# Spectral filter with fused feed-forward: six filter-plane transfers, negation on VectorE, joined d remainders, and a tail inverse in four diagonal blocks

## The chip, the cores and the metric

The kernel runs on one core of one Trainium2 chip. The metric is the device time of one execution in microseconds (us), and less is better. A kernel's time is the median of several runs; beside them one execution is profiled, and all durations in this document that belong to single instructions come from profiled executions. The core has a matrix engine (TensorE, in the profile PE, with its weight loads shown apart as PEld), a vector engine (VectorE, DVE), an activation engine (ScalarE, ACT), GpSimd (POOL) and a synchronisation engine (SP). SP and POOL issue the DMA transfers here.

## The reference

The input `A_x` has 2048 rows (s) of 576 numbers (d), in bfloat16. Two layers follow each other:

```
h  = x + irfft2(rfft2(layernorm(x)) * (w_r + i w_i))
h2 = h + (gelu(layernorm(h) @ w_gate) * (layernorm(h) @ w_up)) @ w_down
```

The transform runs over both axes. The filter has 2048 x 289 complex numbers, held as two planes, `A_w_r` and `A_w_i`. The feed-forward part has an inner width of 4608. The result has the shape and type of `x`.

## The kernel before

Rows are split as s = 16 p + c: p is the SBUF partition (128 of them) and c is one of 16 tiles. Everything is written out in one program; a small class `Prog` derives the waits from the keys that each operation reads and writes, and every engine runs its own operations in the order in which they were recorded. For the spectral part that order is written out by hand in three strings (`SEQ1`, `SEQF`, `SEQ`), in which each word stands for one operation with its number.

**Stage A (`SEQ1`).** The 16 tiles of x arrive in five transfers. Statistics of the first layer norm are made per tile on VectorE (`B`, L464) or ScalarE (`S`, `Q`). The table ATB is scaled by the row's inverse deviation (`x`), and TensorE multiplies (`M`, L520) for five chunks k of d. Chunks 0 to 3 are 128 wide; they use the sums and differences of the two halves of d, for which POOL negates one half (`n`). Chunk 4 holds the remainder of d, two pieces of 32 numbers (256 to 287 and 544 to 575); its matmuls give 32 output partitions each, so that 64 partitions of U are filled, and the other 64 are zeroed once on POOL (L450). `E` copies a PSUM bank into U.

**Filter stage (`SEQF`).** There are 16 groups of rows of the spectrum, in the order of `GORD`. For each group:

- `D` (L574) makes the transform along d, six matmuls of 288 columns into two PSUM banks (odd and even columns of the spectrum, o = 0 and 1), three for each: two with 128-wide chunks and one with the remainder, 128 rows of which 64 are zero. One eviction on ScalarE writes CUS with columns interleaved.
- `B` (L584) finishes the transform along s: four matmuls, one eviction to YS on ScalarE.
- `T` (L594) multiplies on VectorE with the filter. For the complex product the filter buffer WS holds three planes per group: minus w_i, w_r and w_i.
- `Z` (L600, L603) adds the products on VectorE: 256 columns to ZS, the remaining 32 to ZR.
- `V` (L610) starts the inverse along s with four matmuls and an eviction to V on ScalarE.
- `R` (L620) does the same for the 32 remaining columns of up to four groups at once, and copies the result to VR, group by group, 32 partitions at a time (L565, VectorE and once ScalarE).

The filter planes come in 36 transfers, all issued by SP (`w_loads`, L428): for each plane, two halves of the groups, and in each half one transfer for every fourth row, with 72, 63 or 36 KB. The whole w_i plane is issued before w_r, behind the tables FT, BT and VT. POOL makes the negated plane, group by group (L632), once stage A's last scaled table is there, and then zeroes VR (L635). Behind that on POOL's queue stands the first load of gate weights, which has a buffer of its own and waits for nothing else; the other two gate and up slots share their memory with WS and wait for the last product.

**Inverse (`SEQ`).** For each of the first 8 tiles of rows `I` (L684) makes the inverse along d: for two halves h three matmuls of 288 columns, i = 0 and 1 from V, and i = 2, the tail, from VR. VR has 16 groups of 8 values, that is 128 weight columns, in which every 32-partition block is filled only for its own four groups; the rest is zero, and one matmul over 128 rows sums what is needed. `N` (L723) finishes the inverse along s and adds to x. The second layer norm follows, and TensorE transposes the first tiles (L777).

**Feed-forward.** Four blocks of 512 rows: gate and up (L824), 36 steps with 64-row matmuls on the two halves of the array, then down (L874), eight half-width passes of 36 matmuls. In the first block's down part the inverse of the other 8 tiles is done: `def_i` (L841) ahead of each half-width pass, eight matmuls of 144 columns, four from V and four from VR, and `def_n` (L855) at f == 22. Between them stand one ScalarE copy (L844) and four VectorE operations (L848 to L851).

Banks of PSUM for D, B, V and R are given out by the small loop from L550.

Of the kernel before, what the change touches and what calls it, by code (L numbers as in the profile page):

```python
# [12 lines left out]
NZ = 5  # L13
NVZ = 15
# [9 lines left out]
SEQ1 = """k14 B0 B1 v0 Q2 S2 B3 q0 v1 n0 n2 c0 q1 S4 x0D c1 M0 E1A B6 E0A Q4 B5 B7 x1P v2 E2D n1 B8 E3A E4A k104 M1 q2 c2 B9 Q10 E5A E7A n3 v3 S10 B12 E6A q3 c3 x2P B11 k202 M2 E9A x3P Q13 v4 E12A E8A q4 n4 B14 c4 B15 E10A E11A S13 E13D M3 E14A E15A v5 x4P E16D q5 E17A c5 E18A M4 n5 x5D E20D E19A E22D E21A M5 E23D E24A E25A E27A E26D E29A E28D""".split()  # L24
ACT_TILES = tuple(int(w[1:]) for w in SEQ1 if w[0] == "Q")
SEQF = """D0 D1 B0 D2 D3 T0 B1 D4 T1 B2 Z0 Z1 D5 T2 Z2 B3 D6 T3 B4 T4 D7 B5 Z4 D8 Z3 V0 B6 T5 Z5 T6 V1 B7 V3 Z6 T7 D9 R0 B8 D10 V2 Z7 D11 T8 B9 V6 B10 Z8 T9 R1 B11 V4 Z9 D12 D13 V5 T10 B12 T11 Z10 V7 B13 Z11 T12 T13 D14 R2 V9 D15 B14 V8 B15 Z12 V10 Z13 V13 V11 T14 Z14 V12 V14 T15a T15b Z15b Z15a R3 V15 R4""".split()
RENG = [['dve', 'dve', 'dve', 'dve'], ['dve', 'dve', 'dve', 'dve'], ['dve', 'dve', 'dve', 'act'], ['dve', 'dve', 'dve'], ['dve']]
# [13 lines left out]
def build_tables():  # L41
# [7 lines left out]
    T = {}  # L49
    n1 = np.arange(128)[:, None]  # L50
# [17 lines left out]
    I = I.reshape(4, 16, 2, 16, 128).transpose(1, 0, 2, 3, 4)  # L68
# [12 lines left out]
    fr = np.zeros((6, 128, 2, HK))  # L81
    dr = np.concatenate([np.arange(256, 288), np.arange(544, 576)])
    for o, kk in enumerate((k2o, k2e)):
        for h, fn in enumerate((np.cos, np.sin)):
            for t in range(2):
                fr[3 * o + t, :, h] = fn(ang(np.arange(128 * t, 128 * t + 128), kk))
            fr[3 * o + 2, 0:64, h] = fn(ang(dr, kk))
# [220 lines left out]
def _build(nc, A_x, A_w_r, A_w_i, B_w_gate, B_w_up, B_w_down, out):  # L308
# [16 lines left out]
    WS = sb.alloc("WS", [128, NG, 3, KW], BF16)  # L325
# [3 lines left out]
    VR = sb.alloc("VR", [128, NT, 2, NG, 8], BF16)  # L329
# [38 lines left out]
    FT = sb.alloc("FT", [128, 6, 2 * HK], BF16)  # L368
# [47 lines left out]
    x_load(0, 0, 2)  # L416
    x_load(1, 2, 4)
    atb_load(0, 0, 4)
    x_load(2, 4, 8)
    atb_load(1, 4, 8)  # L420
    x_load(3, 8, 12)
    x_load(4, 12, 16)
    atb_load(2, 8, 16)
    P.dma(SP, FT[:, :, :].rearrange("p a b -> p (a b)"), dram["FTAB"][:, :], "ft", w=["FT"])
    P.dma(SP, BT[:, :, :, :].rearrange("p a b c -> p (a b c)"), dram["BTAB"][:, :], "bt", w=["BT"])
    P.dma(SP, VT[:, :, :, :].rearrange("p a b c -> p (a b c)"), dram["VTAB"][:, :], "vt", w=["VT"])

    def w_loads(pl, hf, eng):  # L428
        g0, g1 = ((1, 9), (9, 16))[hf]
        src = (A_w_r, A_w_i)[pl]  # L430
        o = []
        for jj in range(4):
            o.append((WS[jj:64:4, g0:g1, 1 + pl, :], 1 + (16 * jj + g0) * K2, [[128 * K2, 16], [K2, g1 - g0], [1, K2 - 1]], jj))
            o.append((WS[64 + jj:128:4, g0:g1, 1 + pl, :], 1 + (64 + 16 * jj + 16 - g0) * K2, [[128 * K2, 16], [-K2, g1 - g0], [1, K2 - 1]], 4 + jj))
        if hf:
            for p0 in range(2):
                o.append((WS[64 * p0:64 * p0 + 64, 0, 1 + pl, :], 1 + 64 * p0 * K2, [[128 * K2, 16], [16 * K2, 4], [1, K2 - 1]], 8 + p0))
        return [lambda d=d, off=off, ap=ap, h=h: P.dma(eng, d, bass.AP(src.tensor, off, ap), f"w{pl}{hf}", w=[("W", hf, pl, h)]) for d, off, ap, h in o]

    for f in w_loads(1, 0, SP) + w_loads(1, 1, SP) + w_loads(0, 0, SP) + w_loads(0, 1, SP):  # L440
        f()
    GORD = list(range(1, NG)) + [0]
    wkeys = [[("W", hf, pl, h) for pl in range(2) for h in range(8 + 2 * hf)] for hf in range(2)]
# [6 lines left out]
    P.op(POOL, lambda g: g.memset(U[64:128, 4, :, :, :], 0.0), w=["Uz"])  # L450
# [56 lines left out]
    def a_mm(i):  # L507
        c0, c1 = GROUPS[i]
        for k in AORD:
            b = a_bank(i, k)  # L510
            for c in range(c0, c1):
                o = 128 * (c - c0)
                if k == 4:
                    parts = [(XO[:, c, 256 + 288 * h:288 + 288 * h], 32 * h, 32 * h + 32, True, True) for h in range(2)]
                else:
                    d0 = 128 * (k // 2)
                    x2 = XN[:, c, d0:d0 + 128] if k % 2 else XO[:, c, 288 + d0:416 + d0]
                    parts = [(XO[:, c, d0:d0 + 128], 0, 128, True, False), (x2, 0, 128, False, True)]
# [4 lines left out]
    def a_ev(n, eng):  # L523
        i, k = n // 5, AORD[n % 5]
        c0, c1 = GROUPS[i]
        n, b, w = c1 - c0, a_bank(i, k), 64 if k == 4 else 128
# [18 lines left out]
    P.alias([("XN", c) for c in range(NT)], [("V", g, c) for g in range(NG) for c in range(2)])  # L545
    uk = [[("U", i, k) for i in range(len(GROUPS))] + (["Uz"] if k == 4 else []) for k in range(5)]
# [4 lines left out]
    for t, w in enumerate(SEQF):  # L551
# [5 lines left out]
        elif k in "VR":  # L557
            b = min((6, 7) if ("D", LAST) not in FB else range(8), key=lambda b: used[b])
            used[b] = t + 1
        else:  # L560
            continue
# [6 lines left out]
    def st_D(i, eng=ACT):  # L568
        g = GORD[i]
        b0, s3 = FB["D", i], i % 3  # L570
        for o in range(2):
            b = b0 + o
            for m, us in enumerate((1 - o, 3 - o, 4) if o == 0 else (4, 1 - o, 3 - o)):
                P.op(PE, lambda t, b=b, m=m, us=us, o=o, g=g: t.matmul(bank(b, 0, 128, 0, 2 * HK), U[:, us, g, :, :], FT[:, 3 * o + (2 if us == 4 else us // 2), :], start=(m == 0), stop=(m == 2)),  # L574
                    r=uk[us] + ["FT"], w=[("PS", b)])
        ev(eng, CUS[:, s3, :, :].rearrange("p a (j r) -> p r a j", r=2), banks(b0, 2, 2 * HK).rearrange("p r (a j) -> p r a j", a=2),
           [("PS", b0), ("PS", b0 + 1)], [("CU", s3)])
# [10 lines left out]
    def st_T(i, q0=0, q1=KW, hs=(0, 1)):  # L588
        g, sl = GORD[i], i % 2
# [5 lines left out]
             r=[("Y", sl), ("Wn", i)] + wkeys[0 if 1 <= g < 9 else 1], w=[("T", sl, h) for h in hs])  # L595

    def st_Z(i, hs=(0, 1)):
# [3 lines left out]
        if 1 in hs:  # L601
            q, j = (i // 4 % 2, i % 4) if i < LAST else (0, 0)
# [3 lines left out]
    def st_V(i, b=6, eng=ACT):  # L606
        g, z3, sp_ = GORD[i], i % NZ, 1 if GORD[i] == 0 else 0
        for c in range(2):
            for zp in range(2):
                P.op(PE, lambda t, b=b, c=c, zp=zp, sp_=sp_, z3=z3: t.matmul(bank(b, 0, 128, 256 * c, 256 * c + 256), ZS[:, z3, zp, c:256:2], VT[:, sp_, zp, :],  # L610
                                                                            start=(zp == 0), stop=(zp == 1)), r=[("Z", z3), "VT"], w=[("PS", b)])
        for k0, k1, e in ((0, 4, eng),) if eng is not None else ((0, 2, ACT), (2, 4, ACT)):
            ev(e, V[:, :, k0:k1, g, :].rearrange("p n k e -> p k n e"), bank(b, 0, 128, 128 * k0, 128 * k1).rearrange("p (k n e) -> p k n e", k=k1 - k0, n=16),
               [("PS", b)], [("V", g, k) for k in range(k0 // 2, k1 // 2)])

    def st_R(q, engs, b=7):
        js = [i for i in range(4 * q, 4 * q + 4) if i < LAST] if q < 4 else [LAST]
        sp_, n = (1, 32) if q == 4 else (0, 32 * len(js))
        for zp in range(2):
            P.op(PE, lambda t, b=b, zp=zp, n=n, q=q, sp_=sp_: t.matmul(bank(b, 0, n, 0, 256), ZR[:, q % 2, zp, 0:n], VT[:, sp_, zp, :], start=(zp == 0), stop=(zp == 1)),  # L620
                 r=[("ZR", q % 2, j) for j in range(len(js))] + ["VT"], w=[("PS", b)])
        for j, i in enumerate(js):
            ev(engs[j], VR[32 * j:32 * j + 32, :, :, GORD[i], :].rearrange("p n k e -> p k n e"), bank(b, 32 * j, 32 * j + 32, 0, 256).rearrange("p (k n e) -> p k n e", k=2, n=16),
               [("PS", b), "Vz"], [("V", GORD[i], 2)])
# [6 lines left out]
    for i in range(NG):  # L631
        P.op(POOL, lambda v, g=GORD[i]: v.tensor_scalar(WS[:, g, 0, :], WS[:, g, 2, :], -1.0, 1.0, op0=ALU.mult, op1=ALU.mult),  # L632
             r=[k for k in wkeys[0 if 1 <= GORD[i] < 9 else 1] if k[2] == 1] + [("ATS", NT - 1)], w=[("Wn", i)])
        if i == NVZ:
            P.op(POOL, lambda g: g.memset(VR[:, :, :, :, :], 0.0), w=["Vz"])  # L635
    for w in SEQF:
        i = int(w[1:].rstrip("abc"))
        if w[0] == "D":
            st_D(i)
        elif w[0] == "B":  # L640
            st_B(i)
# [7 lines left out]
        elif w[0] == "V":  # L649
            st_V(i, FB["V", i], ACT if i < LAST else None)  # L650
# [21 lines left out]
    vk = [[("V", g, c) for g in range(NG)] for c in range(3)]  # L672
    vkeys = vk[0] + vk[1] + vk[2] + ["Vz"]
# [8 lines left out]
    def i_mm(c, h, i):  # L682
        b, kt = SLOT["I", c] + h, 2 * i + h
        P.op(PE, lambda t, b=b, h=h, i=i, kt=kt, c=c: t.matmul(bank(b, 0, 128, 0, KW), (V[:, c, kt, :, :] if kt < 4 else VR[:, c, kt - 4, :, :]), DT[:, 3 * h + i, 0:KW],  # L684
                                                              start=(i == 0), stop=(i == 2)), r=vk[i] + ["DT"], w=[("PS", b)])
# [151 lines left out]
    def def_i(c):  # L837
        for o in range(2):
            for t_ in range(2):
                for i, ch in enumerate((o, 2)):  # L840
                    P.op(PE, lambda t, o=o, t_=t_, i=i, ch=ch, c=c: t.matmul(bank(2 + o, 0, 128, HK * t_, HK * t_ + HK), (V[:, c, 2 * ch + t_, :, :] if ch < 2 else VR[:, c, t_, :, :]),  # L841
# [106 lines left out]
```

## Time and profile before

| What | Value |
|---|---|
| Median of 3 runs | 496.52 us (495.99 to 497.1) |
| Profiled execution | 496.66 us |
| Its span, first to last instruction | 494.9 us |
| TensorE busy | 486.1 us (98%) |
| VectorE, ScalarE, GpSimd busy | 192.4, 158.9, 34.6 us |
| Stage A | to 20.0 us |
| Filter stage | 20.0 to 52.44 us |
| First product with the filter | 27.26 us |
| Inverse and second layer norm | 52.44 to 64.77 us |
| Gate and up, first block | 64.77 to 134.8 us |
| Down with deferred inverse | 134.8 to 176.2 us |

A row of the groups gives the source line, the engine, the operation, the tile written and those read, partitions x elements, the count, then busy time and the mean of one in ns, then the engine's idle time ahead of it and what ended it. For matmuls, 128*32 means 128 rows of the array and 32 weight columns. Starts are recorded; matmul ends are modelled, so a matmul's "mean" contains its way through the array, and the step from one start to the next is the better measure of its cost. A row of the chain or timeline gives the start, the length and what ran.

### The profile page before, as it was taken

How to read it: one execution, taken by the hardware profiler on the slowest of the kernel's cores; microseconds unless marked ns; L12 is line 12 of the kernel's file. 1: busy time of each engine (PE TensorE's matmuls, PEld its weight loads, DVE VectorE, ACT ScalarE, POOL GpSimd, SP SyncE). 2: the span in 40 equal slices, each digit the busy share in tenths (PEclk: the TensorE clock that was granted, in tenths of full speed). 3: DMA queues.
4: the chain of work that ended last, by engine and by line, in shares of the span. 5: the costliest groups of instructions: out<-in, count | busy, mean ns of one | idle time of the engine just before them, and what ended most of it. 6: DMA issues, size and time to landing. Idle time of an engine off the chain costs nothing.

```text
span 494.9 us, 9880 instructions
## 1 busy us (share of the span) xinstructions
PE 486.1 (98%) x4338; PEld 288.1 (58%) x4338; DVE 192.4 (39%) x418; ACT 158.9 (32%) x300; POOL 34.6 (7%) x53
## 2 busy tenths in 40 slices
PE   7999999999999999999999999999999999999998
PEld 3767655555588854444477744444677544444775
DVE  6679743444365644433311144333211233333111
ACT  6989865232312243232300033232100132233000
POOL 5750701000000010000000000000000000000000
DMA  8666898411000062000000001000000000000000
GB/s 276 163 188 215 277 350 275 178 25 27 4 13 13 19 191 60 19 9 1 1 13 19 18 15 23 19 1 1 7 19 12 14 1 1 1 1 2 12 19 19
DMA packets 27164, 31.26 MB, mean 63 GB/s; under 512 B 11664, under 2 KB 20112, under 8 KB 27120
## 3 DMA queue, kind: packets, MB, share of 16 engines
q1 hardware_dynamic: 24224, 18.68, 13.0%
q0 software_dynamic: 2896, 11.95, 7.1%
q8 instruction: 34, 0.56, 0.5%
q14 instruction: 10, 0.08, 0.1%
HBM read 26.28 MB, written 2.36 MB: 58 GB/s over the span
## 4 chain that ended last, share of the span: by engine, by line
PE 88%; DVE 4%; issue 1%; ACT 0%; DVEq 0%
PE PS L824 57%; PE PS L874 29%; DVE TP L594 1%; DVE VR L565 1%; PE PS L841 1%; PE PS L684 1%; PE PS L723 1%; DVE ZS L600 1%; DVE XO L726 0%; PE PS L855 0%; DVE ZR L603 0%; PE PS L610 0%; DVE HN L757 0%; PE PS L777 0%; DVE TM L734 0%
## 5 line engine op out<-in xcount | busy, mean ns | idle before, releaser
L824 PE MATMUL PS<-HT,WG 64*128 64x512 bf16 x2106 | 228.5, 376 | 0.0
L824 PEld LDWEIGHTS PS<-HT,WG 64*128 64x128 bf16 x2106 | 107.3, 94 | 119.8 <-issue 1.0
L833 ACT ACTIVATE GL<-PS 128x512 bf16<-128x512 f32 x144 | 85.9, 597 | 257.3 <-PE PS L824 243.4
L834 DVE TENSOR_TENSOR AT<-GL,PS 128x512 bf16<-128x512 bf16 x144 | 98.9, 687 | 175.0 <-ACT GL L833 175.0
L874 PE MATMUL PS<-WD,AT 128*128 128x288 bf16 (+2 forms) x1152 | 144.3, 286 | 0.0
L874 PEld LDWEIGHTS PS<-WD,AT 128*128 128x128 bf16 x1152 | 110.8, 98 | 30.7 <-ACT GL L833 1.3
L877 DVE TENSOR_TENSOR OS<-PS,XO 128x288 bf16<-128x288 f32 (+2 forms) x32 | 14.6, 457 | 100.3 <-PE PS L874 100.3
L824 PE MATMUL PS<-HT,WGX 64*128 64x512 bf16 x486 | 53.4, 376 | 0.0
L824 PEld LDWEIGHTS PS<-HT,WGX 64*128 64x128 bf16 x486 | 23.7, 94 | 28.8
L714 ACT ACTIVATE JD<-XO 128x576 bf16<-128x576 bf16 x8 | 5.5, 683 | 28.5 <-DVE XO L858 28.5
L594 DVE TENSOR_TENSOR TP<-YS,WS 128x1152 bf16<-128x1152 bf16 (+2 forms) x17 | 11.8, 715 | 6.8 <-DMA WS<-in_A_w_r_dram 6.7
L574 PE MATMUL PS<-FT,U 128*128 128x288 bf16 x96 | 14.1, 286 | 0.1
L565 ACT ACTIVATE CUS<-PS 128x576 bf16<-128x576 f32 x16 | 13.5, 862 | 0.5 <-PE PS L574 0.4
L565 ACT ACTIVATE YS<-PS 128x576 bf16<-128x576 f32 x16 | 11.3, 705 | 2.3 <-DVE TP L594 2.2
L520 PE MATMUL PS<-ATS,XO 128*128 128x128 bf16 (+1 forms) x128 | 10.1, 221 | 1.7 <-POOL XN L534 1.1
L584 PE MATMUL PS<-CUS,BT 128*128 128x288 bf16 x64 | 10.5, 286 | 1.2 <-ACT YS L565 0.9
L464 DVE BATCH_NORM_STATS2 ST<-XO 128x6 f32<-128x288 bf16 x24 | 9.3, 438 | 4.5 <-DMA XO<-in_A_x_dram 4.5
L574 PEld LDWEIGHTS PS<-FT,U 128*128 128x128 bf16 x96 | 9.1, 98 | 2.9 <-ACT CUS L565 0.4
L520 PEld LDWEIGHTS PS<-ATS,XO 128*128 128x128 bf16 (+1 forms) x128 | 7.4, 97 | 4.7 <-POOL XN L534 1.6
L610 PE MATMUL PS<-VT,ZS 128*128 128x256 bf16 x64 | 9.0, 273 | 1.1 <-DVE VR L565 0.5
L565 ACT ACTIVATE V<-PS 128x512 bf16<-128x512 f32 (+1 forms) x17 | 10.0, 639 | 0.3 <-PE PS L610 0.2
L757 DVE TENSOR_SCALAR HN<-XO,TM,RS 128x576 bf16<-128x576 bf16 (+1 forms) x32 | 10.0, 361 | 0.0
(77 smaller groups left out, 215.0 us busy)
## 6 DMA issues: line engine op xcount, KB each, us to landing
WD<-in_B_w_down_dram POOLq DMA_DIRECT2D x9, 576.0 KB, 21.4
WG<-in_B_w_gate_dram POOLq DMA_DIRECT2D x4, 1152.0 KB, 9.7
WG<-in_B_w_up_dram SPq DMA_DIRECT2D x4, 1152.0 KB, 7.9
out_dram<-OS SPq DMA_DIRECT2D x30, 72.0 KB, 1.6
XO<-in_A_x_dram SPq DMA_DIRECT2D x3, 576.0 KB, 7.4
WGX<-in_B_w_gate_dram POOLq DMA_DIRECT2D x1, 1152.0 KB, 6.9
WGX<-in_B_w_up_dram SPq DMA_DIRECT2D x1, 1152.0 KB, 10.8
HT<-HN SPq DMA_TRANSPOSE x60, 2.4
```

What stands on the lines that cost most here:

```text
L464: P.op(DVE, lambda v, c=c, h=h: v.bn_stats(ST1[:, c, h, :], XO[:, c, 288 * h:288 * h + 288]), r=[("X", c)], w=[("ST1", c, h)])
L520: P.op(PE, lambda t, b=b, lhs=lhs, p0=p0, p1=p1, s=s, e=e, o=o, c=c: t.matmul(bank(b, p0, p1, o, o + 128), lhs, ATS[:, c, :], start=s, sto ...
L565: fn = (lambda v: v.tensor_copy(dst, src)) if eng == DVE else (lambda a: a.activation(dst, src, ACTF.Copy))
L574: P.op(PE, lambda t, b=b, m=m, us=us, o=o, g=g: t.matmul(bank(b, 0, 128, 0, 2 * HK), U[:, us, g, :, :], FT[:, 3 * o + (2 if us == 4 else u ...
L584: P.op(PE, lambda t, b=b, tb=tb, m=m, s3=s3, sp_=sp_: t.matmul(bank(b, 0, 128, 0, KW), BT[:, sp_, tb, :], CUS[:, s3, m, :], start=(m == 0) ...
L594: P.op(DVE, lambda v: v.tensor_tensor(TP[:, sl, :, :, q0:q1], y4, w4, op=ALU.mult), r=[("Y", sl), ("Wn", i)] + wkeys[0 if 1 <= g < 9 else ...
L757: P.op(eng, lambda v, c=c, hs=hs, o0=o0, o1=o1, x0=x0, x1=x1: v.tensor_scalar(HN[:, hs, o0:o1], XO[:, c, x0:x1], TM[:, 1, c:c + 1], RS2[:, ...
L824: op = P.op(PE, lambda t, h0=h0, kt=kt, wt=wt, b=b, s=(not second and j == 0), e=(second and j == n - 1): t.matmul(bank(b), wg_tile(slot)[ ...
L833: P.op(ACT, lambda a: a.activation(GL[:, s2, :], bank(b0), ACTF.Gelu_apprx_tanh), r=[("PS", b0)], w=[("GL", s2)])
L834: P.op(DVE, lambda v: v.tensor_tensor(AT[:, f, :], GL[:, s2, :], bank(b0 + 1), op=ALU.mult), r=[("GL", s2), ("PS", b0 + 1)], w=[("AT", f)])
L874: P.op(PE, lambda t, b=b, d0=d0, d1=d1, f=f, p=p: t.matmul(bank(b, 0, 128, 0, d1 - d0), AT[:, f, 128 * p:128 * p + 128], WD[:, f, d0:d1], ...
L877: P.op(DVE, lambda v, b=b, d0=d0, d1=d1, p=p, c=c: v.tensor_tensor(OS[:, p % 2, d0:d1], bank(b, 0, 128, 0, d1 - d0), XO[:, c, d0:d1], op=A ...
```

## The change

- **Six transfers.** Each filter plane is loaded in three: partitions 0 to 63 for slots 0 to 15, partitions 64 to 127 for slots 16 down to 1, and partitions 0 to 63 for slot 16. WS has 17 slots; the groups in their order use slots 1 to 16. SP issues w_i before w_r within each part, ahead of VT.
- **Negation on VectorE.** The words `w0` to `w3` negate w_i for four groups at a time. POOL no longer negates the plane. Each product waits for all six transfers and for its negation.
- **One pair of row halves.** Stage A writes the d remainder twice, to partitions 0 to 63 and 64 to 127 (four 32-column matmuls per tile instead of two). D then begins with two matmuls on 64 rows, lower for o = 0 and upper for o = 1, and goes on with four full ones. FT has five planes instead of six, and POOL no longer zeroes part of U. The D eviction writes in order and reads PSUM interleaved.
- **Tail in four diagonal blocks.** V and VR hold the groups in the order `GSLOT`, and ITAB is permuted to fit. VR holds only each block's own four groups, a quarter of its former size, without zeroes; R copies all groups of a set in one operation. The tail of the inverse, `I` at i = 2 and `def_i` at ch = 2, becomes four matmuls with 32 rows and 32 weight columns, from partitions 32 j to output partitions 32 j.
- **Order and engines.** `SEQ1`, `SEQF` are new; six statistics passes on ScalarE instead of eight. D0, B10 and V14 are evicted by VectorE; R2 and R3 by ScalarE. V15 goes to two banks.

```diff
-    for i in range(NG):
-        P.op(POOL, lambda v, g=GORD[i]: v.tensor_scalar(WS[:, g, 0, :], WS[:, g, 2, :], -1.0, 1.0, ...), ...)
-        if i == NVZ:
-            P.op(POOL, lambda g: g.memset(VR[:, :, :, :, :], 0.0), w=["Vz"])
+    def st_w(i):
+        g0, g1 = 4 * i + 1, 4 * i + 5
+        P.op(DVE, lambda v: v.tensor_scalar(WS[:, g0:g1, 0, :], WS[:, g0:g1, 2, :], -1.0, None, op0=ALU.mult), r=wkeys[1], w=[("Wn", 4 * i + k) for k in range(4)])
...
+    def w_load(pl, part):
+        src = (A_w_r, A_w_i)[pl].tensor
+        if part == 0:
+            dst, ap = WS[0:64, 0:NG, 1 + pl, :], bass.AP(src, 1, [[128 * K2, 16], [K2, 64], [1, K2 - 1]])
+        elif part == 1:
+            dst, ap = WS[64:128, NG:0:-1, 1 + pl, :], bass.AP(src, 1 + 64 * K2, [[128 * K2, 16], [K2, 64], [1, K2 - 1]])
+        else:
+            dst, ap = WS[0:64, NG, 1 + pl, :], bass.AP(src, 1, [[128 * K2, 16], [16 * K2, 4], [1, K2 - 1]])
+        P.dma(SP, dst, ap, f"w{pl}{part}", w=[("W", pl, part)])
+    for part in range(2):
+        for pl in (1, 0):
+            w_load(pl, part)
+    for pl in (1, 0):
+        w_load(pl, 2)
...
     def st_D(i, eng=ACT):
+        for m in range(3):
+            for o in range(2):
+                p0, p1 = (0, 128) if m else (64 * o, 64 * o + 64)
+                us, fs = (2 * m - 1 - o, 2 * o + m - 1) if m else (4, 4)
...
-                    parts = [(XO[:, c, 256 + 288 * h:288 + 288 * h], 32 * h, 32 * h + 32, True, True) for h in range(2)]
+                    parts = [(XO[:, c, 256 + 288 * (h % 2):288 + 288 * (h % 2)], 32 * h, 32 * h + 32, True, True) for h in range(4)]
...
     def i_mm(c, h, i):
+        for p0, p1 in [(0, 128)] if i < 2 else [(32 * j, 32 * j + 32) for j in range(4)]:
+            lhs = V[:, c, kt, :, :] if i < 2 else VR[p0:p1, c, h, :, :]
...
     def def_i(c):
+                    for p0, p1 in [(0, 128)] if ch < 2 else [(32 * j, 32 * j + 32) for j in range(4)]:
+                        lhs = V[:, c, 2 * ch + t_, :, :] if ch < 2 else VR[p0:p1, c, t_, :, :]
```

## The prediction

> **What bounds the kernel now.** I read the chain of work that ended last in order of time, then busy time by stage, the waits, both DMA queues, and groups by shape.
>
> The chain (start us, length us, what):
>
> ```profile
> 40.56 0.41 DVE VR L565
> ...
> 49.91 0.74 DVE TP L594 x2
> ...
> 52.44 1.63 PE PS L684 x12
> ...
> 64.77 70.11 PE PS L824 x648
> 134.88 0.61 PE PS L841 x8
> 135.48 2.69 PE PS L874 x22
> ```
>
> After 64.77 us the chain is TensorE without a gap, so each nanosecond added to its stream there is added to the end. From 27.26 to 52.3 us the chain lies mostly on VectorE (products L594, sums L600/L603, remainder copies L565), then on TensorE in the inverse (L684, L723). Busy time of each engine in the head, filter, inverse and first gate/up stage:
>
> ```profile
> 20.00:27.26 7.26, 7.00 (x58) 5.17 (x56) 0.56 (x2) 5.52 (x9) 6.14 (x14) 1.00 0.43 91
> 27.26:52.44 25.18, 22.66 (x182) 16.57 (x181) 24.54 (x63) 23.71 (x43) 5.86 (x6) 1.00 0.62 194
> 52.44:64.77 12.33, 11.82 (x100) 8.61 (x101) 9.92 (x34) 10.19 (x24) 7.91 (x11) 1.00 1.02 364
> 64.77:134.81 70.04, 70.04 (x649) 36.55 (x649) 27.35 (x51) 26.94 (x46) 1.28 (x2) 1.00 0.42 136
> ```
>
> Columns after the length: PE, PEld, DVE, ACT, POOL. In the filter stage all three compute engines are nearly full, DVE most; in the inverse PE has 0.51 us of slack; then none. VectorE does nothing from 20.5 to 27.26 because of one wait, whose cause is SP's issuing, 18 small transfers per plane at about 0.64 us each:
>
> ```profile
> DVE TP L594 <- DMA WS<-in_A_w_r_dram: 6.7, 1, 6.7
> ```
> ```profile
> 19.51 12.57 SPq L218 DMA_DIRECT2D WS<-in_A_w_r_dram  x18
> ```
>
> The matmuls to be split, by shape, and what stage A shows of a change of array shape:
>
> ```profile
> L684 PE MATMUL PS<-DT,VR 128*128 128x288 bf16 x16 | 4.5, 286 | 0.0
> L841 PE MATMUL PS<-DP,VR 128*128 128x144 bf16 x32 | 4.8, 226 | 0.0
> ```
> ```profile
> 7.47 0.22 PE L520 MATMUL PS<-ATS,XO 128*128 128x128 bf16 x1
> 7.53 0.22 PE L520 MATMUL PS<-ATS,XN 128*128 128x128 bf16 x1
> 7.68 0.29 PE L520 MATMUL PS<-ATS,XO 128*32 128x128 bf16 x4
> ```
>
> Full matmuls start 0.056 us apart; the first with 32 columns starts 0.149 after the last full one. The trace's own starts give 95 to 99 ns beyond streaming at each of the 20 changes that no other wait disturbs: 128x128 to 128x32 (7) and back (6), 64x128 to 128x128 (4, one of them at the first L841), 128x128 to 64x128 (3). The matmul after a change back starts a further 10 ns late.
>
> **What the Trainium skill says.** "TensorEngine Tiling (Array Packing)", Key Properties: changing the tiling mode, not just the tile, drains TensorE. The trace agrees, 95 to 99 ns. "TensorE: Matmul & The Clock Gate", Part 3: tiles on different row groups run together, about 4 ns apart. The trace agrees for two: 3 to 4 ns between the 128x32 ones of a pair, 3 to 20 ns between 64-row halves; four diagonal blocks it does not show. "SBUF — State Buffer", Door 1: a transfer to 64 partitions reaches 8 of 16 ports, 196 GB/s at 1 MiB. The new transfers have 64 partitions or fewer. The nearest measurement is the drain of queued plane rows at 14.5 to 16.5 us, about 402 rows of 576 B per us = 232 GB/s, both halves mixed. "DMA: Bandwidth & Descriptors", Issuing engines are not separate DMA queues: SP's and POOL's transfers share the engines. The trace agrees: while POOL's gate load flowed (32 to 35 us, 337 GB/s) the last two w_r transfers, issued at 30.8 and 31.5, waited and landed at 37.3 and 38.1.
>
> **Part by part.**
>
> *Transfers.* 36 plane issues become 6; at 0.65 us SP is through them by about 10.5 us instead of 32. The bound becomes the data: 4,224 rows, 2.43 MB. FT and BT land near 14.4; by then perhaps 900 rows have come (525 before, plus the time of VT's 256 KB, now queued behind, and FT's 72 KB less). The other 3,300 need 8.2 us at 402 rows/us or 9.7 at 196 GB/s: 22.6 to 24.1, and 0.5 us to complete. But POOL loses 16 negations (8.2 us with gaps) and the 3.5 us memset, so its queue comes to the first gate load after x_neg 5, at about 17.5 us instead of 30.1; 1.33 MB start flowing some 1.7 us later and take 3.3 us at 400 GB/s, shared with the rows. So the last plane lands between 23.1 (no sharing) and 28 (all 3.3 us, low rate); I take 26.5. VT follows within a microsecond, and the inverse tables soon after (41.8 us before).
>
> *Negation on VectorE.* w0 stands ahead of T0 and waits for the whole w_i plane. Four planes at once, 1,152 elements: the nearest row is tensor_scalar 128x576 at 425 ns, so 0.45 to 0.6, I take 0.5. T0 starts at 27.0 (23.6 to 28.5) against 27.26: the large stall mostly remains. Queued behind w0 are only products, for which ACT's YS and then PE wait, as before.
>
> *VectorE after T0.* Before: 25.7 us almost without a gap. New: products 16 x 0.68 = 10.9, sums 16 x 0.53 = 8.5, remainder copies 3 x 0.43 = 1.3 instead of 6.4, w1 to w3 1.5, B10 0.7, V14 0.65: 23.6. So 2.1 of work goes. ACT sheds two evictions there and takes R2, R3 at 0.38. The CUS eviction now reads PSUM strided and writes in order; the trace has no such form: 0.65 us (YS row, same size) to 0.2 slower than today's 0.86 mean. At 9 evictions after T0 that is 1.8 us on about 21, still under VectorE.
>
> *Forward d remainder.* Per D: two full matmuls (0.244) become a 64-row pair (0.126), but two shape changes (0.194) and the 10 ns: +0.086, x16 = +1.4 us of PE, 0.8 of it after T0 (9 D's). PE there goes from about 20.6 to 21.5 us, under VectorE's 23.6, so hidden; without that cover it costs the 0.8. In stage A four 128x32 pieces per tile replace two, together in the array: nothing but a few ns each; PE is not its bound. The U memset (1.8 us) hid under the x loads. ACT there has 6 statistics passes and 25 copies for 8 and 22; a shorter stage A goes into the wait for the planes.
>
> Filter sum: 0.3 earlier plus 2.1 less, with 0.6 given back as three full engines wait for each other: -1.8 (from -5 to +1).
>
> *Inverse tail.* Each of 16 remainders in the inverse (L684 row) and 32 in the deferred inverse (L841 row) becomes an excursion to four 32x32 blocks: in 0.095, blocks as long as the one matmul plus 3 x 0.004, out 0.097, 0.010 after: 0.214 us. Inverse: 16 x 0.214 = 3.4, less 0.4 of PE's slack: +3.0. Deferred: 32 x 0.214 = 6.85, all in a stage with no PE gap: +6.9. If blocks start 20 ns apart, as some halves do, 48 x 0.048 = 2.3 more. The EB/QB/YB chain to the f == 22 matmuls shifts along and stays in its cover.
>
> Sum: -1.8 + 3.0 + 6.9 = +8.1 on the profiled span 494.9, 503.0. The profiled execution took 496.66 (1.76 outside the span), the median is 496.52: 504.6.
>
> **The rivals.**
> *Four blocks one after another*: they write one PSUM bank. Then 3 x 0.122 x 16 = 5.9 and 3 x 0.062 x 32 = 6.0 more: 516.5. For it: unseen here; against it: the pairs seen in one bank (128x32) run together.
> *Planes no earlier, filter not shorter*: the rows crawl behind the gate load, T0 at 28.5, filter +1: 507.4. For it: the w_r transfers at 37 us.
> *No drain for the blocks* (other side): small weights load behind running full matmuls, an excursion costs 0.012. Then D gains instead of losing (0.2 of it after T0), inverse and deferred pay 48 x 0.012 = 0.6: -1.8 - 0.2 + 0.6 = -1.4, or with the planes at 23.6 and the filter 5 shorter -4.6: 491.9 to 495.1. It decides when an excursion costs under about 0.046 us, (1.8 + 0.4 of slack)/48. Against it: every shape change in the trace pays 95 ns or more.
>
> **How the numbers follow.** Main case 0.73 (504.6, own range 500.5 to 508.5), serial blocks 0.07, late planes 0.10, no drain 0.10. The range 500.3 to 509 holds most of the main case (0.70) and of the late planes (0.09). About 0.2% (1 us) is what measurement tells from no change: no drain gives faster 0.08 and same 0.02, the main case's far tail 0.01 of same; slower 0.89.
>
> **What would show it.** Each L841 group of a deferred half taking 1.35 us instead of 0.5, gaps of 0.095 at each 32-row block, the inverse 15.3 us long instead of 12.3, the first product near 27 behind an SP queue empty since 11, first inverse matmul near 50.6, gate/up blocks still 70.04. Wrong if the blocks start without a gap, or if the planes land by 23.5 and the filter gives 5 us.

## The result and the profile after

The changed kernel takes 509.47 us (median) against 496.54 us: ratio 1.0258 [1.0238, 1.0278], slower. The prediction was 504.6 us with a range of 500.3 to 509.0, so the direction is right and the time lies just above the range. One execution of the changed kernel had TensorE at about a quarter of its speed throughout (1,805 us); the profile shown here is that of the next measurement of the same kernel (509.52 us, ratio 1.0261 [1.0246, 1.0276]). Its span is 507.3 us, in an execution of 509.12 us.

Busy time by stage, after: head up to the landing of the planes, filter from there, inverse, first gate and up block. Columns after the length are PE, PEld, DVE, ACT and POOL, each with its count, then TensorE's granted clock, the DMA share and GB/s.

```profile
20.00:30.36 10.36, 8.35 (x62) 4.31 (x59) 1.25 (x4) 4.67 (x8) 0.00 (x0) 1.00 1.10 276
30.36:55.76 25.40, 23.31 (x176) 15.73 (x177) 22.20 (x58) 21.98 (x41) 0.74 (x1) 0.93 0.27 96
55.76:70.36 14.60, 14.52 (x150) 7.74 (x149) 9.64 (x33) 10.69 (x25) 8.58 (x13) 1.00 1.02 351
70.36:140.47 70.11, 70.11 (x649) 36.62 (x649) 27.41 (x51) 26.95 (x46) 1.28 (x2) 1.00 0.40 128
```

The head has become longer, not shorter; the clock in the filter stage is 0.93, which no stage of the kernel before shows. The chain of work that ended last, after (start, length, what):

```profile
17.21 13.02 DMA WS<-in_A_w_i_dram
30.36 0.47 DVE WS L604
30.95 0.77 DVE TP L599
...
55.93 2.22 PE PS L693 x24
...
140.47 1.36 PE PS L852 x20
141.83 2.80 PE PS L885 x22
...
146.59 1.25 PE PS L852 x20
```

L604 is the negation, L599 the product, L693 and L852 are the inverse's matmuls in I and in the deferred half (L684 and L841 before). A deferred group before:

```profile
140.15 0.50 PE PS L841 x8
```

These 0.50 us have become 1.25, and the 22 matmuls of L885 behind the group take 2.80 instead of 2.69, because the last change back falls into them. The last w_i transfer, the small one for slot 16, lands 13 us after SP came to it. From 32.45 us on the chain lies on TensorE, where before it lay mostly on VectorE up to the inverse. Steps by stage, with the prediction's own terms:

| Stage | before | after | difference | predicted |
|---|---|---|---|---|
| first product at | 27.26 | 30.95 | +3.7 | -0.3 |
| filter, first product to first inverse matmul | 25.2 | 24.8 | -0.4 | -1.5 |
| inverse to first gate and up matmul | 12.3 | 14.6 | +2.3 | +3.0 |
| gate and up, first block | 70.0 | 70.0 | 0 | 0 |
| down with deferred inverse | 41.4 | 48.2 | +6.9 | +6.9 |
| sum on the span | 494.9 | 507.3 | +12.4 | +8.1 |

(The differences are taken before rounding.) The two tail terms are near what was predicted. What failed is the first line, and with it the second. The waits of the filter stage, after (engine, line waited for: us in total, times, longest):

```profile
DVE WS L604 <- DMA WS<-in_A_w_i_dram: 8.4, 1, 8.4
ACT YS L569 <- DVE TP L599: 5.2, 1, 5.2
...
PE PS L589 <- ACT YS L569: 4.0, 1, 4.0
```

All three engines stand still for the planes, TensorE for some 4 us. SP's queue, after (start, length, DMA issue):

```profile
6.01 0.69 SPq L222 DMA_DIRECT2D WS<-in_A_w_i_dram  x1
6.74 3.76 SPq L222 DMA_DIRECT2D WS<-in_A_w_r_dram  x1
10.54 3.77 SPq L222 DMA_DIRECT2D WS<-in_A_w_i_dram  x1
14.35 2.82 SPq L222 DMA_DIRECT2D WS<-in_A_w_r_dram  x1
17.21 3.24 SPq L222 DMA_DIRECT2D WS<-in_A_w_i_dram  x1
20.50 0.93 SPq L222 DMA_DIRECT2D WS<-in_A_w_r_dram  x1
```

Six issues instead of 36, but four of them hold SP for 2.8 to 3.8 us while earlier rows are still queued, three of the large ones (1,024 rows) and one of the two small ones (64 rows): SP is through at 21.4 us, not at 10.5. POOL's queue, after:

```profile
17.16 1.51 POOL L222 DMA_DIRECT2D WG<-in_B_w_gate_dram  x2
```

POOL comes to the gate load at 17.16 us, with the planes still on their way. What the DMA engines moved from 10 to 34 us, 0.6 us a number, first after, then with that gate load held back (an experiment below):

```profile
GB/s 414 401 389 371 286 206 205 205 204 202 203 205 205 229 237 189 193 205 196 205 212 267 225 363 387 381 359 304 244 221 180 307 303 392 403 406 402 386 379 382
```
```profile
GB/s 401 402 392 383 360 213 205 207 202 197 203 218 212 231 213 204 202 201 198 194 184 240 218 255 363 334 351 409 410 398 386 379 390 384 380 315 334 380 386 342
```

While plane rows alone flow (13 to 22 us) the rate is 205 GB/s, about 350 rows a microsecond. That is close to the 196 GB/s at 1 MiB which the Trainium skill's "SBUF — State Buffer", Door 1, gives for 64 partitions, and not the 232 GB/s that the smaller transfers of the kernel before had reached. No run changes the partitions alone, so the partitions as the reason are not shown. The gate load's first packet comes at 21.9 us.

### The profile page after: what moved, and what is told of

It reads as the page before. It is cut to its first block, busy times and chain, and to the rows that moved or that the text cites. A ratio compares the mean times of both kernels' runs of the same rounds, so it can differ in the third digit from the quotient of the medians.

```text
span 1803.5 us, 10170 instructions
## 1 busy us (share of the span) xinstructions
PE 1799.1 (100%) x4513; PEld 641.3 (36%) x4514; DVE 191.5 (11%) x409; ACT 161.5 (9%) x297; POOL 22.9 (1%) x36
## 4 chain that ended last, share of the span: by engine, by line
PE 100%; issue 0%; POOL 0%; DVE 0%; DVEq 0%; POOLq 0%
PE PS L833 59%; PE PS L885 29%; PE PS L579 2%; PE PS L589 2%; PE PS L518 2%; PE PS L619 1%; PE PS L693 1%; PE PS L503 1%; PE PS L732 1%; PE PS L852 1%; PE PS L866 0%; PE PS L786 0%; PE PS L631 0%; POOL ZD L409 0%; DVE OS L888 0%
## 5 line engine op out<-in xcount | busy, mean ns | idle before, releaser
L833 PE MATMUL PS<-HT,WG 64*128 64x512 bf16 x2106 | 865.7, 1100 | 0.0
L885 PE MATMUL PS<-WD,AT 128*128 128x288 bf16 (+2 forms) x1152 | 533.5, 738 | 0.0
L833 PEld LDWEIGHTS PS<-HT,WG 64*128 64x128 bf16 x2106 | 239.6, 218 | 622.6 <-issue 622.6
L885 PEld LDWEIGHTS PS<-WD,AT 128*128 128x128 bf16 x1152 | 256.8, 225 | 270.0 <-issue 267.9
L833 PE MATMUL PS<-HT,WGX 64*128 64x512 bf16 x486 | 200.9, 1097 | 0.0
L833 PEld LDWEIGHTS PS<-HT,WGX 64*128 64x128 bf16 x486 | 54.7, 216 | 144.4 <-issue 144.4
L888 DVE TENSOR_TENSOR OS<-PS,XO 128x288 bf16<-128x288 f32 (+2 forms) x32 | 14.6, 457 | 430.6 <-PE PS L885 430.6
L579 PE MATMUL PS<-FT,U 128*128 128x288 bf16 (+1 forms) x96 | 37.7, 628 | 0.0
L589 PE MATMUL PS<-CUS,BT 128*128 128x288 bf16 x64 | 33.6, 747 | 0.0
L619 PE MATMUL PS<-VT,ZS 128*128 128x256 bf16 x64 | 29.3, 682 | 0.0
L518 PE MATMUL PS<-ATS,XO 128*128 128x128 bf16 (+1 forms) x160 | 29.3, 394 | 0.0
L579 PEld LDWEIGHTS PS<-FT,U 128*128 128x128 bf16 (+1 forms) x96 | 10.3, 135 | 25.9 <-issue 23.5
L619 PEld LDWEIGHTS PS<-VT,ZS 128*128 128x128 bf16 x64 | 13.6, 213 | 13.3 <-issue 13.0
L693 PE MATMUL PS<-DT,V 128*128 128x288 bf16 x32 | 17.5, 679 | 0.0
L599 DVE TENSOR_TENSOR TP<-YS,WS 128x1152 bf16<-128x1152 bf16 (+2 forms) x17 | 12.2, 720 | 40.5 <-ACT YS L569 40.5
## 6 DMA issues: line engine op xcount, KB each, us to landing
WD<-in_B_w_down_dram POOLq DMA_DIRECT2D x9, 576.0 KB, 21.5
```

What stands on the lines that cost most here:

```text
L518: P.op(PE, lambda t, b=b, lhs=lhs, p0=p0, p1=p1, s=s, e=e, o=o, c=c: t.matmul(bank(b, p0, p1, o, o + 128), lhs, ATS[:, c, :], start=s, sto ...
L579: P.op(PE, lambda t, b=b0 + o, m=m, us=us, fs=fs, g=g, p0=p0, p1=p1: t.matmul(bank(b, 0, 128, 0, 2 * HK), U[p0:p1, us, g, :, :], FT[p0:p1, ...
L589: P.op(PE, lambda t, b=b, tb=tb, m=m, s3=s3, sp_=sp_: t.matmul(bank(b, 0, 128, 0, KW), BT[:, sp_, tb, :], CUS[:, s3, m, :], start=(m == 0) ...
L619: P.op(PE, lambda t, b=b[c], c=c, zp=zp, sp_=sp_, z3=z3: t.matmul(bank(b, 0, 128, 256 * c, 256 * c + 256), ZS[:, z3, zp, c:256:2], VT[:, s ...
L693: P.op(PE, lambda t, b=b, h=h, i=i, lhs=lhs, p0=p0, p1=p1: t.matmul(bank(b, p0, p1, 0, KW), lhs, DT[p0:p1, 3 * h + i, 0:KW], start=(i == 0 ...
L833: op = P.op(PE, lambda t, h0=h0, kt=kt, wt=wt, b=b, s=(not second and j == 0), e=(second and j == n - 1): t.matmul(bank(b), wg_tile(slot)[ ...
```

## The experiments

Theory A is the prediction's: each excursion to the blocks costs two changes of array shape, 0.214 us, and nothing else. Its rival B: the blocks cost more than their changes of shape, and the tails hold nearly all of the loss. Theory C: TensorE's clock drops in the wait for the planes. Theory D: what is left is that wait, made longer by the early gate load, with C's drop behind it. All ratios are to the kernel before, run on the same chip beside each.

**The changed kernel again.**

> The changed kernel again, unaltered, for a profile at full TensorE clock. Theory A (each excursion into the four 32x32 blocks costs two drains, about 0.21 us, and the blocks run together): eight matmul groups of the deferred inverse 1.36 us each instead of 0.50, inverse stage 15.3 us, the filter stage then has to hold the remaining 4.8 us of the measured loss, so the first inverse matmul would stand near 55, not 50.6. Theory B (the blocks are dearer than predicted, for instance one after another): deferred group 1.9 to 2.1 us, inverse stage 19 to 21 us, and the filter stage ends near 50.6. Theory C (the wait for the planes lets the TensorE clock drop): a stretch near 20 to 28 us with matmul steps twice as long.

Measured 509.52 us, as told above: the first deferred group takes 1.36 us, as A says, the first inverse matmul comes at 55.8, and a stretch at half clock is there too, but at 33.0 to 36.4 us, after the wait.

**Tails as one full matmul in the changed kernel.** Tails take stand-in weights from V, so that no change of shape remains; the tails' contribution is left out.

```
-        for p0, p1 in [(0, 128)] if i < 2 else [(32 * j, 32 * j + 32) for j in range(4)]:
+        for p0, p1 in [(0, 128)]:
-            lhs = V[:, c, kt, :, :] if i < 2 else VR[p0:p1, c, h, :, :]
+            lhs = V[:, c, kt % 4, :, :]
```
(and the same in `def_i`)

> The changed kernel with every tail of the inverse, in both inverse and deferred inverse, as one full 128x128 matmul that takes weights from V as a stand-in: the tail's true contribution is left out, all else stays. Theory A: 10.3 us less than the changed kernel, about 499, which leaves 2.6 above the kernel before to the filter stage. Theory B: 14 to 15 us less, about 495, faster than the kernel before.

Measured 501.06 us, 1.0085 [1.0067, 1.0103]: 8.5 us less than the changed kernel, nearer A's 10.3 than B's 14 to 15. In the profiled execution, the fastest of four (499.31 us), the inverse takes 12.4 us and the deferred group its 0.50 us again, while the first product stays late, at 30.2.

**Tails as blocks in the kernel before.** Nothing else of the change; the blocks read stand-in columns of VR, so wrong groups are summed.

```
+        for j, (p0, p1) in enumerate([(0, 128)] if i < 2 else [(32 * j, 32 * j + 32) for j in range(4)]):
+            lhs = V[:, c, kt, :, :] if i < 2 else VR[p0:p1, c, h, 4 * j:4 * j + 4, :]
```

> The kernel before with its tails alone cut into four diagonal 32x32 blocks, 32 contiguous columns of VR each as a stand-in, so the tail is summed over the wrong groups; nothing else altered. Theory A: 9.9 us more than the kernel before, 506.4. Theory B: 14 to 21 us more, 510 to 517.

Measured 505.79 us, 1.0189 [1.0172, 1.0206]: +9.2 us. By the profile the inverse has 2.3 of it (14.6 against 12.3) and the down part with its eight deferred halves 6.9 (48.2 against 41.4). Both directions agree, so the tails are some 9 of the 12.9 us, and B falls. The chain in this kernel has the changed kernel's group lengths (1.36 and 2.80 in the first half):

```profile
136.47 1.36 PE PS L845 x20
137.83 2.80 PE PS L878 x22
```

Recorded starts in the changed kernel give the parts of one excursion of L852 (full matmuls of 144 columns start 62 ns apart): full to first block 166 ns, blocks 3 to 4 ns apart, last block to the next full matmul 164 ns. From full to full that is 340 ns instead of 125, so 0.215 us each, against 0.214 predicted. Groups by shape, changed kernel (busy us, mean ns):

```profile
L852 PE MATMUL PS<-DP,VR 32*32 32x144 bf16 x128 | 7.7, 232 | 0.0
L693 PE MATMUL PS<-DT,VR 32*32 32x288 bf16 x64 | 4.8, 292 | 0.0
```

The mean of a block is as long as that of a full matmul (226 and 286 ns before); the busy time is not four times as long because the four run at once, in one PSUM bank.

**Fewer excursions.** The changed kernel, complete, with the tails of a tile behind each other: 8 excursions in the inverse instead of 16, and 8 in the deferred part instead of 32, for which the deferred sums get four banks.

```
-        for h in range(2):
-            for i in range(3):
-                i_mm(c, h, i)
+        for h, i in ((0, 0), (0, 1), (1, 0), (1, 1), (0, 2), (1, 2)):
+            i_mm(c, h, i)
...
-        for o in range(2):
-            for t_ in range(2):
-                for i, ch in enumerate((o, 2)):
+        for i in range(2):
+            for o in range(2):
+                for t_ in range(2):
+                    ch = (o, 2)[i]
```

> The changed kernel, complete, with the block matmuls gathered: in the inverse both halves' full matmuls first and then both tails, in the deferred inverse four full matmuls in four banks and then the four tails. Excursions go from 16 to 8 and from 32 to 8. Theory A: 24 x 0.20 + 8 x 0.20 = 6.4 us less than the changed kernel, 503.1. If the cost sits in the blocks themselves and not in entering and leaving, it stays at 508 to 509.5.

Measured 503.36 us, 1.0138 [1.0123, 1.0153]: 6.2 us less for 32 excursions less, 0.19 each. By the profiles the deferred part gives 4.7 us (24 excursions, 0.19 each) and the inverse 1.1 (8 excursions); 0.5 is a first product that came earlier in this execution. A deferred group takes 0.61 us:

```profile
144.89 0.61 PE PS L852 x20
```

With the last change back, which falls into the matmuls behind the group here too (2.80 us), one excursion of 16 blocks costs 0.22 us, as much as one of four. That is what A says: the price goes with the number of excursions, not with the blocks in them.

**The gate load held back.** In the changed kernel POOL's first gate load waits for all planes; it is needed only at 64 us or later.

```
-            P.dma(eng, tile[:, 4 * o:4 * o + 4, :], ..., f"wgu{o}{j}{slot}", w=[("WG", slot, o)])
+            P.dma(eng, tile[:, 4 * o:4 * o + 4, :], ..., f"wgu{o}{j}{slot}",
+                  r=wkeys[0] + wkeys[1] if (j, slot, o) == (0, 0, 0) else [], w=[("WG", slot, o)])
```

> The changed kernel, complete, with one thing altered: POOL's first gate load waits until all six plane transfers have landed. Theory D (the gate load, which now starts at 17 us instead of 30, takes the DMA engines from the plane rows, and the idle time that follows lets the TensorE clock drop to half for some 4 us): the planes land near 24.6 (4,224 rows at the 351 per us seen before the gate load begins), the first product at 25.3 instead of 30.95, no stretch at half clock, the first inverse matmul at 48 to 49 instead of 55.8: 7 us less than the changed kernel, 502.5. Rival E (the 64-partition transfers alone make the planes late): first product near 30, 509.

Measured 503.44 us, 1.0137 [1.0122, 1.0152]: 6.1 us less. Landing of the four large plane transfers, from the trace:

```
                    w_i lower  w_r lower  w_i upper  w_r upper   last small one
changed kernel        17.39      20.15      23.61      30.03        30.42
gate load held        17.56      20.20      23.36      25.71        26.07
```

Three land alike, and the fourth 4.3 us earlier without the gate load. In the changed kernel only some 370 rows were left at 23 us. From then to 27 us they came at 33 to 64 a microsecond, and the gate load's packets of 4,608 bytes at 51 to 80: packet against packet that is one order, but in bytes the rows had a tenth or so. From 26 us on SP's own tables share the time as well. The negation and the load, gate held (idle time and its cause in brackets):

```profile
26.01 0.46 DVE L604 TENSOR_SCALAR WS<-WS 128x1152 bf16<-128x1152 bf16 x1 [4.40 <-DMA WS<-in_A_w_i_dram]
```
```profile
26.80 1.51 POOL L222 DMA_DIRECT2D WG<-in_B_w_gate_dram  x2 [9.79 <-DMA WS<-in_A_w_r_dram]
```

The first product comes at 26.60 instead of 30.95 (4.35 us). A further 1.5 us lie after it: the filter takes 23.3 us instead of 24.8. In this stretch TensorE has no gap at all, while VectorE is busy for 21.7 us:

```profile
26.60:49.91 23.31, 23.31 (x188) 15.99 (x187) 21.67 (x57) 21.47 (x41) 2.26 (x3) 1.00 0.45 152
```

The chain that ended last lies on TensorE in this run from 13.6 us to the gate and up matmuls, so the planes are no longer on it.

**TensorE kept at work in the wait.** Those 1.5 us have a candidate. Busy time in two stretches of the changed kernel, the eighth number being the clock:

```profile
28.30:33.00 4.70, 0.71 (x6) 0.31 (x4) 2.51 (x6) 1.26 (x3) 0.00 (x0) 1.00 1.04 359
33.00:36.40 3.40, 3.40 (x16) 1.69 (x16) 3.30 (x9) 2.88 (x5) 0.00 (x0) 0.51 1.01 350
```

After 4.3 us without a matmul TensorE has half its clock for 3.41 us. The changed kernel with fillers on TensorE ahead of D6:

```
         elif w[0] == "D":
+            if i == 6:
+                idle_ft(24, FB["D", 6])
             st_D(i, DENG[i])
```

> The changed kernel with 24 filler matmuls on TensorE ahead of D6, so that it works through part of its wait for the planes (28.2 to 32.4 us); what they write is overwritten. If the half clock from 33.0 to 36.4 us comes from that idle time and costs what the D and B matmuls of that stretch took longer, it is gone and the time is 507.8, 1.7 below the changed kernel. If the stretch is bound by VectorE whatever the clock, 509.5.

Measured 507.54 us, 1.0216 [1.0202, 1.023], below the changed kernel's interval. The clock stays at 1:

```profile
33.00:36.40 3.40, 2.63 (x20) 1.61 (x21) 3.40 (x10) 3.33 (x7) 0.00 (x0) 1.00 0.91 299
```

and the filter takes 23.3 us from its first product, as with the gate load held. In the profiled execution, the slowest of five (508.95 us), the planes happened to land 1.3 us later. In this stage, over the thirteen profiles used here, each with a gap of 3.1 us or more between matmul starts (3.1, 3.8, 3.9 and 4.3 us) has one such half-clock stretch of 3.41 us, and none with gaps up to 2.5 us has it. The Trainium skill's "TensorE: Matmul & The Clock Gate", Part 1, says the clock halves after an idle window of about 3.4 us. The traces agree in kind, but here a gap of 3.1 us was enough.

**Both repairs.** Grouped tails and the held gate load.

> Both repairs together, complete: block matmuls gathered, and the gate load held back until the planes are there. If the two losses are independent, 503.4 - 7 = 496.4, level with the kernel before. If the gain in the filter stage is given back in the inverse (waiting for the later tables or weights), 498 or more.

Measured 497.87 us, 1.0025 [1.0014, 1.0035]: the two gains nearly add up (6.2 and 6.1, together 11.6). The repaired kernel still doesn't reach the one before.

**The d remainder undone.** The kernel with the held gate load, with D's remainder over 128 rows again instead of a row pair (odd and even halves are mixed, so the sums differ).

```
-                p0, p1 = (0, 128) if m else (64 * o, 64 * o + 64)
+                p0, p1 = (0, 128)
```

> As the run with the late gate load, with the pair of row halves in D undone: six full 128-row matmuls, the remainder over all 128 rows, so that odd and even columns are mixed in it (that part is wrong). Prediction's step: the pair costs 0.086 us more TensorE time per group, hidden under VectorE: the same as that run within 0.8 us. If TensorE has become the bound of the filter stage, 1.0 to 1.4 us less.

Measured 503.04 us, 1.0126 [1.0109, 1.0143], 0.4 us below 503.44, with intervals that overlap. The times alone don't tell the two apart; the profiles do. One D, with the pair (the kernel with the held gate load) and then without it:

```profile
27.33 0.82 PE PS L579 x6
```
```profile
30.44 0.73 PE PS L579 x6
```

The pair costs 0.09 us a D, as the sum said (0.086), and it does not hide: from the first product to the first inverse matmul this run takes 22.55 us instead of 23.31, which is the 0.8 that the prediction named for a pair without cover. Only 0.4 us arrive at the end because in this execution the first product came 0.4 us later (27.00).

**The wait for the planes in the kernel before.** The order of its plane transfers only: first halves of both planes, then second halves.

```
-    for f in w_loads(1, 0, SP) + w_loads(1, 1, SP) + w_loads(0, 0, SP) + w_loads(0, 1, SP):
+    for f in w_loads(1, 0, SP) + w_loads(0, 0, SP) + w_loads(1, 1, SP) + w_loads(0, 1, SP):
```

> The kernel before, complete, with the order of its 36 plane transfers altered alone: first half of the groups of w_i, first half of w_r, then the second halves. If the arrival of the first planes sets the filter stage, as both theories hold, the first product starts at about 23.4 instead of 27.26 and the kernel takes 492.7, faster than both. Rival: the second halves, whose last transfers landed at 38 behind the gate load, become the wait, at the ninth product: 494.5. If VectorE's own work were the only bound, nothing would change: 496.5.

Measured 496.53 us, 1.0003 [0.9995, 1.0012]. In the profile the first product came 3.7 us earlier (23.59), and the first inverse matmul 0.7 us later. On POOL the second eight negations wait for w_i's second half, the zeroing of VR stands behind them, and the first remainder copy waits for that:

```profile
37.02 1.72 DVE L565 CAST VR<-PS 32x256 bf16<-32x256 f32 x4 [1.41 <-POOL VR L635]
```

**That wait taken away too.** The same, and on POOL the zeroing of VR after the eighth negation (`NVZ = 7` instead of 15).

> The kernel before with the planes in the order w_i and w_r first halves, then second halves, and on POOL the 3.5 us memset of VR moved ahead of the second eight negations, into the 4.8 us that POOL waits there for w_i's second half. If the first remainder copy's wait for that memset (37.0 us) is what took the 3.7 us back that the earlier T0 gave, T0 comes at 23.6, the filter takes 25.2 us after it, and the time is 492.9, 0.7% below the kernel before. If the stretched VectorE and POOL instructions of that stretch take it back whatever waits, 496.5.

Measured 495.58 us, 0.9983 [0.9976, 0.999], the fastest kernel of this study, 0.9 us under the one before. The copy starts at 35.02 without a wait, and the first product comes at 22.95, 4.3 us earlier than before. But 3.0 us are given back: the filter takes 28.1 us after its first product, not 25.2. So the copy's wait wasn't all of it. Busy time in the filter's second part:

```profile
36.00:51.10 15.10, 12.96 (x105) 9.72 (x106) 14.72 (x39) 14.19 (x27) 1.50 (x3) 1.00 0.65 210
```

VectorE is nearly full there and TensorE is not; up to 36 us it was TensorE that had no gap (13.02 of 13.04 us). Two causes are at hand for the 3.0 us. TensorE had its own work to do first. And while POOL negated the second eight groups (26.4 to 32.0 us), VectorE's short sums (L603) took up to 0.41 us instead of 0.18; added up, its products and sums took some 1.6 us longer than in the kernel before, where they ran after the negations. That is the stretching named in the second forecast. No run separates the two, so neither is shown.

**The planes split in the repaired kernel.** Grouped tails and held gate load, with first halves of both planes first, in 36 transfers again; the first eight products wait for the first halves alone.

```
-             r=[("Y", sl), ("Wn", i)] + wkeys[0] + wkeys[1], w=[("T", sl, h) for h in hs])
+             r=[("Y", sl), ("Wn", i)] + whalf[i > 7][0] + whalf[i > 7][1], w=[("T", sl, h) for h in hs])
```

> The grouped tails and the held gate load, and the planes cut again: first halves of w_i and w_r (slots 1 to 8, 16 transfers of 128 rows), then the second halves; the first eight products wait for the first halves only, w2, w3 and the later products for the second. No plane work is on POOL. If the wait for the planes is a wait for rows that the first products don't use, T0 comes at 23.6 as it did with the plane order changed in the kernel before, the filter takes 23.3 us after it, the first inverse matmul comes at 47.2 instead of 50.5, and the time is 494.6, about 0.4% below the kernel before. If the filter gives the gain back as it did there, because other work than POOL's negation holds its end, 497.9.

Measured 501.59 us, 1.01 [1.0084, 1.0116], slower than unsplit and above both forecasts, though the first product comes at 23.07. VT stands behind the planes on SP's queue, with 36 issues of nearly 0.7 us each ahead of it, and the first V waits for it; TensorE stands still for 3.1 us and again gets half its clock:

```profile
PE PS L621 <- DMA VT<-c_vtab: 2.8, 1, 2.8
```
```profile
30.51 0.58 SPq L222 DMA_DIRECT2D VT<-c_vtab  x1
```

**VT between the halves.** The same with VT's issue moved up.

> The split planes once more, with VT's transfer moved from behind the planes to between their halves. If V0's wait for VT (to 33.5 us) is all that lengthened the filter there, T0 comes near 23.2, the filter takes 23.3 us after it as in the two kernels with the held gate load, the first inverse matmul comes at 46.5 to 47.2, and the time is 494.2, 0.5% below the kernel before. If other waits come up in VT's place (the second halves land only at 32, products 8 to 15 need them), 497.9 or more.

Measured 497.49 us, 1.0018 [1.0012, 1.0025], 4.1 us better, but only 0.4 us below the unsplit kernel (1.0025 [1.0014, 1.0035], so the intervals overlap) and not 3.7. First product at 22.63, first inverse matmul at 49.24: 26.6 us of filter, where 23.3 were expected. Busy time up to 36 us, and in the unsplit kernel its filter's first half:

```profile
22.63:36.00 13.37, 13.37 (x107) 8.57 (x106) 9.51 (x24) 12.20 (x21) 1.51 (x2) 1.00 0.55 154
```
```profile
27.14:38.80 11.66, 11.50 (x92) 7.43 (x90) 10.79 (x29) 10.58 (x20) 1.51 (x2) 1.00 0.88 305
```

With an early first product TensorE is busy without a gap and ScalarE for 12.2 of 13.4 us, while VectorE has time left (9.5): the planes no longer bound this stretch. TensorE and ScalarE had spent the wait for the planes on D, B and evictions that must be done anyway. From 20 us to the first inverse matmul PE is busy for 29.1 of 29.2 us here, and for 30.2 of 30.45 in the unsplit kernel. The chain that ended last is TensorE alone from 20.0 us to 56.1. That reads as why an earlier first product is worth so little here; no run takes work off TensorE behind an early first product, so it isn't shown by itself. It doesn't carry over to the reordered kernel before, whose filter ends on VectorE.

## Why the prediction was right and wrong

**Right: what the tails cost.** The step "0.214 us" an excursion measured 0.215. The blocks start 3 to 4 ns apart, as taken from the pairs, though none of these differed in rows and columns at once. The deferred inverse has +6.9 us for +6.9. The rival of serial blocks is out, and so is the one without a drain. The inverse's +3.0 measured +2.3, because the slack was mis-sized: "0.4 of PE's slack" was read from the busy share, which counts modelled matmul ends as busy. From start to start, the steps of this stage that exceed their columns by more than 0.13 us have 1.3 us of idle time before and 0.2 after, so 1.1 of the 3.4 us fell into it.

**Wrong: the planes.** The step that failed is "So the last plane lands between 23.1 (no sharing) and 28 (all 3.3 us, low rate); I take 26.5." The last landed at 30.4, and the first product at 30.95 lies outside even the late-planes rival's 28.5. Its terms, one by one. The rows by 14.4 us, "perhaps 900", were 870 to 890. The rate was the low one, 205 GB/s, and the 402 rows/us that spoke for better came from transfers whose two halves alternated. Without the gate load the end is 26.1, not the 24.6 of the low rate: from 22 us on the rows fell from 340 to 296, 222 and 109 a microsecond, while SP's own VT, DT and IT, which the sum left out, came in. And the gate load, priced as at most its own 3.3 us, cost 4.3 us with only some 370 rows left: the rows got about a tenth of the bytes while it flowed, so a load that shares cannot be priced by its own length. That POOL would come to the load at about 17.5 us was right (17.16), but its packets began to flow 4.7 us later and not 1.7. So the consequence was right in kind, not in size.

**Wrong: the filter's length, and what bounds it.** The sum makes the filter 1.5 us shorter from the first product, so 23.6 us. At full clock it measured 23.3 (with the gate load held, and with fillers), but the reason given does not hold, so the near hit is luck. VectorE, said to need 23.6 us of work, was busy for 21.7. TensorE, said to need 21.5 and to stay "under VectorE's 23.6, so hidden", was busy for 23.3 without a gap: among other things ten D's lie behind the first product and not nine, and all their pairs count. The changed kernel took 24.8; the term missing from the sum is the half clock, 1.5 us, which follows from TensorE's 4.3 us without work, so from the same late planes. "SP is through them by about 10.5 us" was wrong too (21.4): an issue was costed by the small transfers of the kernel before. It cost nothing that can be seen, since rows were queued all that time.

Together: first product 3.9 us later than predicted, filter 1.2 longer, inverse 0.7 shorter, deferred part as predicted: that is, within rounding, the 4.3 us from 503.0 to 507.3. The w0 term (0.5) measured 0.47, the new CUS eviction 0.65 us, the low end of its span.

**The same error from the other side.** The sum treated an earlier first product as a gain of its full length (range to -5). First products 3.7 to 4.5 us earlier brought 0 to 0.9 us (the kernel before reordered, the same with the zeroing moved, and the split planes with VT between).

## What to carry to other kernels

Count changes of array shape, not matmuls: here each pair of changes cost 0.21 us of TensorE, with four blocks between or sixteen, so that small blocks pay only if many stand behind each other, and in a stage without a TensorE gap it all reaches the end. When work is taken off an engine that also issues transfers, ask what it will now issue earlier, and into which transfer that falls; and price the loser by its rows' share of the engines, not by the other's length. A stage in which three engines are nearly full has no safe cover: a cost hidden under one engine came out in full when another became the bound. A stall at which the other engines work ahead can be worth far less than its length.

## What was not expected of the hardware

- A gap of 3.1 us or more between matmul starts gave 3.41 us at half clock; gaps up to 2.5 us gave none.
- With plane rows queued ahead, the issue of a 1,024-row transfer held SP for 2.8 to 3.8 us, and that of a 64-row one once for 3.24 us and once for 0.93; the first 1,024-row one, with no plane rows ahead, took 0.69 us.
- Rows of 576 bytes from SP fell from about 350 to 33 to 64 a microsecond while 51 to 80 packets of 4,608 bytes came from POOL's queue.
- VectorE's short sums took up to 0.41 us instead of 0.18 while POOL negated planes; the reason isn't shown.
